# Moving the first value weights behind the last five value tiles in the load queue

## The chip, the cores and the metric

The kernel runs on one core of one Trainium2 chip. The metric is the device time of one execution in microseconds (us). The batches of experiments ran on four chips, each with the kernel before beside it in the same rounds (its medians there are 257.97 to 258.05). Below, "clock" is the TensorE clock that the profile shows as granted, as a share of full speed.

## The reference, cut to what matters

The reference runs windowed attention with block summaries for 4 batches, 8 heads, 768 positions and head size 64, then a gated feed-forward layer on the result.

```python
v_sum = v.reshape(B, H, nb, 32, D).mean(axis=3)          # one mean per block of 32 values
a = softmax([masked q k^T | q k_sum^T + log 32])         # (cut) near keys and block summaries
x = a @ concatenate([v, v_sum])                          # attention out, 3072 x 512
g, val = x @ w_gate, x @ w_val                           # 512 -> 1536 each
ffn = (gelu(g) * val) @ w_out                            # 1536 -> 512
out = x + sigmoid(x @ w_res) * ffn
```

The block means need every value of a batch. So the first attention output, and with it the first feed-forward matmul, cannot be had before the whole of the first batch's v is on the chip.

## The kernel before

Every load goes through one queue, whose DMAs GpSimd (POOL) issues. The loads cast from float32 to bfloat16. v comes as 12 tiles of 64 positions (64 KB each as landed), the gate and value weights as six chunks each (256 KB each as landed).

```python
def v_loads(b, lo=0, hi=NT):
    for t in range(lo, hi):
        nc.gpsimd.dma_start(out=vext[b % 2][0:QT, t, :, 0:D],
                            in_=v[b, :, t * QT:(t + 1) * QT, :].rearrange("h p d -> p h d"))
def load_w(c):                                   # 256 columns, two feed-forward groups
    sl = slice(c * 256, (c + 1) * 256)
    nc.gpsimd.dma_start(out=w_gate[:, :, sl], in_=wg_src[:, :, sl])
    nc.gpsimd.dma_start(out=w_val[:, :, sl], in_=wv_src[:, :, sl])
# ... k, q, then:
v_loads(0, 0, 6)
# ... four selects on POOL
v_loads(0, 6, 7)
load_w(0)
v_loads(0, 7, NT)
# ...
for c in range(1, 6):
    load_w(c)
    if c == 4:
        q_sb[1] = load_q(1, QJ)
# then w_res (residual weights), w_out (three pieces)
```

On TensorE (PE) the head of the program runs in this order. `vsum_mm` makes the block means, two matmuls for each value tile. `keep_warm(n)` issues n matmuls whose result nobody reads.

```python
s_step(0, 2, st)
s_step(0, 3, st, MM2)
vsum_mm(0, vs, 3, 7)                 # tiles 3 to 6
keep_warm(2)
# ...
for hp in range(3):
    av_first(hp, st, ao[hp], 0, BAND)   # attention matmuls, 12 for each head pair
vsum_mm(0, vs, 7, 10)
av_first(3, st, ao[3], 0, BAND)
vsum_mm(0, vs, 10, NT)
nc.vector.tensor_copy(vblk[...], vs[0][...])   # the means; then the rest of attention
# ... then transposes, and the first gate and value matmuls
```

The softmax here doesn't subtract the row's maximum and nothing guards it: scores larger than these inputs give would overflow.

Of the kernel before, what the change touches and what calls it, by code (L numbers as in the profile page):

```python
# [15 lines left out]
def kernel(  # L16
# [11 lines left out]
    nc = tc.nc  # L28
# [11 lines left out]
    NT = S // QT  # L40
# [40 lines left out]
    w_gate = wpool.tile([128, KO, DFF], BF16, name="w_gate")  # L81
    w_val = wpool.tile([128, KO, DFF], BF16, name="w_val")
# [11 lines left out]
    def load_q(half, j):  # L94
        t = qk.tile([TU // j, H, j, D], BF16, tag="q_sb", name="q_sb")
        nc.gpsimd.dma_start(
            out=t.rearrange("p h j d -> p h (j d)"),
            in_=q[0, :, half * TU:(half + 1) * TU].rearrange("h (p j) d -> p h (j d)", j=j))
        return t
# [5 lines that stand above are left out]
# [30 lines left out]
    with tc.manual_schedule():  # L135
# [20 lines left out]
        wg_src = moe_w_gate.rearrange("(ko ki) f -> ki ko f", ki=128)  # L156
        wv_src = moe_w_val.rearrange("(ko ki) f -> ki ko f", ki=128)

        def load_w(c):
            sl = slice(c * 256, (c + 1) * 256)  # L160
            nc.gpsimd.dma_start(out=w_gate[:, :, sl], in_=wg_src[:, :, sl])
            nc.gpsimd.dma_start(out=w_val[:, :, sl], in_=wv_src[:, :, sl])

        nc.vector.memset(warm[:], 0.0)
        nc.vector.memset(ident[:], 0.0)
# [15 lines left out]
        for cols, sign, base in ((slice(0, QT), 1, WIN - 1), (slice(0, QT), -1, WIN - 1),  # L181
# [2 lines left out]
            nc.gpsimd.affine_select(out=m, in_=m, compare_op=ALU.is_ge, fill=-240000.0, base=base,  # L184
                                    pattern=[[-sign, cols.stop - cols.start]], channel_multiplier=sign)
        v_loads(0, 6, 7)
        load_w(0)
        v_loads(0, 7, NT)
        kw_consts(0)
        own_keys(bmat, NT)  # L190
# [1 line left out]
        nc.vector.memset(vext[1][0:QT, :, :, D + 1:VP], 0.0)  # L192


        for c in range(1, 6):
            load_w(c)
            if c == 4:
                q_sb[1] = load_q(1, QJ)
        nc.gpsimd.dma_start(out=w_res[:], in_=moe_w_res.rearrange("(ko ki) f -> ki ko f", ki=128))
        wo_src = moe_w_out.rearrange("(fo ki) f -> ki fo f", ki=128)  # L200
        for c in range(3):
            sl = slice(c * 4, (c + 1) * 4)
# [58 lines left out]
        def vsum_mm(b, vs, lo, hi):  # L261
            for t in range(lo, hi):
                for i in range(2):
                    nc.tensor.matmul(vs[i][96:128, 0:DM // 2], bmat[:, t, :],
                                     vext[b % 2][0:QT, t, 4 * i:4 * i + 4, 0:D],
                                     start=(t == 0), stop=(t == NT - 1))
# [36 lines left out]
        def s_step(u, hp, st, banks=None):  # L303
            if banks:
                s = [p.tile([128, 512], F32, tag=tag, name="s") for p, tag in banks]
            else:
                s2 = ps_s.tile([128, 2, 512], F32, tag="s", name="s")
                s = [s2[:, hh] for hh in range(2)]
            s_mm(u, hp, [x[:, 0:TU] for x in s])
            P = ppool.tile([128, 2, HT, QT], BF16, tag="P", name="P")  # L310
            if banks:
                for hh in range(2):
                    nc.scalar.activation(P[:, hh].rearrange("p t q -> p (t q)"), s[hh][:, 0:TU], AF.Exp,  # L313
                                         scale=scale, bias=bias_t[:])
            else:
                nc.scalar.activation(P.rearrange("p a t q -> p a (t q)"), s2[:, :, 0:TU], AF.Exp,  # L316
                                     scale=scale, bias=bias_t[:])
            if u or hp > 1:
                Pf = P.rearrange("p a t q -> p (a t) q")
                nc.vector.tensor_mul(Pf, Pf, maskt.unsqueeze(1).to_broadcast([128, 2 * HT, QT]))  # L320
            st["P", hp] = P
# [17 lines left out]
        def av_first(hp, st, ao, lo, hi):  # L339
            P = st["P", hp]  # L340
            for sub in range(NSUB):
                for hh in range(2):
                    for e in range(2):
                        t, h = 2 * sub + e, 2 * hp + hh
                        rhs = vblk[lo:hi, h, :] if lo else vext[0][0:hi, t, h, 0:D + 1]
                        nc.tensor.matmul(ao[64 * e:64 * e + 64, sub, hh, :], P[lo:hi, hh, t, :], rhs,
                                         start=(lo == 0 and sub == 0 and hh == 0), stop=(lo > 0),
                                         skip_group_check=True)
# [102 lines left out]
        def keep_warm(n):  # L451
            wp = ps_s.tile([128, 2, 512], F32, tag="s", name="wp")
            for _ in range(n):
                nc.tensor.matmul(wp[:, 0], warm[:, 0:128], warm[:], start=True, stop=True)
# [16 lines left out]
        vs = [ps_t.tile([128, 512], F32, tag="t", name="vs"), ps_o.tile([128, 512], F32, tag="ao", name="vs")]  # L471
# [5 lines left out]
        vsum_mm(0, vs, 0, 3)  # L477
        s_step(0, 2, st)
        s_step(0, 3, st, MM2)
        vsum_mm(0, vs, 3, 7)  # L480
        keep_warm(2)
        gvT = upool.tile([128, FO, TU], BF16, tag="gvT", name="gvT")
        ao = [ps_mm.tile([128, NSUB, 2, D + 1], F32, tag="mm", name="ao") for _ in range(NP)]
        for hp in range(3):
            av_first(hp, st, ao[hp], 0, BAND)
        vsum_mm(0, vs, 7, 10)
        av_first(3, st, ao[3], 0, BAND)
        vsum_mm(0, vs, 10, NT)
        nc.vector.tensor_copy(vblk[96:128, 0:H // 2, 0:D],
                              vs[0][96:128, 0:DM // 2].rearrange("p (h d) -> p h d", d=D))  # L490
        nc.scalar.copy(vblk[96:128, H // 2:H, 0:D],
# [206 lines left out]
```

## Time and profile before

| what | value |
|---|---|
| time | 258.22 us, median of 3 (257.93 to 259.48) |
| profiled span | 256.2 us, clock 1.00 |
| value tiles 7 to 11 land | 17.21, 17.63, 18.05, 18.53, 18.94 us |
| first gate / value weights land | 15.46 / 16.78 us |
| first gate matmul | 22.21 us |

From the page (busy time of an engine and its share; granted clock in 40 slices; the chain that ended last, by engine):

```profile
span 256.2 us, 5835 instructions
PE 250.3 (98%) x2304; PEld 138.9 (54%) x2304; DVE 158.4 (62%) x349; ACT 127.3 (50%) x213; POOL 110.4 (43%) x155
PEclk9999999999999999999999999999999999999999
PE 88%; DMA 5%; ACT 2%; POOL 2%; DVE 2%; issue 1%; POOLq 0%; DVEq 0%
```

PE is the limit almost everywhere, so the 5% of DMA is the interesting part. The chain of waits from 3 to 22 us shows where it lies (start, duration, what; "..." marks rows left out, here and below):

```profile
3.19 7.11 DMA q_sb<-in_q_dram
10.31 0.28 issue
10.59 0.77 POOL w_gate L161
11.36 0.74 POOL w_val L162
12.10 1.34 POOL vext L103 x2
13.44 4.61 DMA vext<-in_v_dram
...
18.09 0.38 PE vs L264 x2
18.47 0.31 PE ao L346 x12
18.78 0.48 PE vs L264 x3
...
19.29 0.45 DVE vblk L489
...
22.21 0.32 PE g L374
```

The value tiles (`vext`) set the pace until 18.05 us. The timeline of PE for the same stretch (start, duration, line, what, shapes, count, idle time before):

```profile
14.80 1.04 PE L264 MATMUL vs<-vext,bmat 64*32 64x256 bf16 x8
16.05 0.59 PE L454 MATMUL wp<-warm 128*128 128x512 bf16 x2 [0.21 <-ACT P L316]
16.57 0.76 PE L346 MATMUL ao<-vext,P 96*64 96x65 bf16 x36
17.26 1.20 PE L264 MATMUL vs<-vext,bmat 64*32 64x256 bf16 x6
18.40 0.38 PE L346 MATMUL ao<-vext,P 96*64 96x65 bf16 x12
18.71 0.65 PE L264 MATMUL vs<-vext,bmat 64*32 64x256 bf16 x4
```

Eight of the block-mean matmuls take 1.04 us at 14.80. The six at 17.26 take 1.20, because they wait inside the row for one landing after another. The view prints idle time from 0.15 us up. A record lasts 0.27 us, so of each wait (0.29 us from tile 7's last matmul to tile 8's first, where the usual spacing is 0.11) almost nothing is left between the records.

A DMA's row on POOL is its issue alone (752 ns for the first value weights, which land 5.4 us after its start). A landing is the start of its issue plus the time to landing in the view of one tile. Here are the first value weights (first pair of lines), then value tiles 7 to 11 (second pair):

```profile
L162 POOL DMA_DIRECT2D w_val<-in_moe_w_val_dram x1: 752/752/752, 11.3 to 11.3; - x1
DMA to landing us min/median/max: 5.4/5.4/5.4
...
L103 POOL DMA_DIRECT2D vext<-in_v_dram x5: 713/722/1042, 12.1 to 15.1; - x5
DMA to landing us min/median/max: 3.9/4.6/5.1
```

The value weights land at 16.78 us, 5.6 us before the first value matmul (22.38) reads them, and the tiles that PE is waiting for queue behind them.

### The profile page before, as it was taken

The numbers are of one execution on the slowest core, as the hardware profiler recorded it, in microseconds if no ns is written. First come the engines' busy times: TensorE is split into PE (matmuls) and PEld (weight loads), VectorE is DVE, ScalarE is ACT, GpSimd is POOL, SyncE is SP. The second block draws the span as 40 slices with busy tenths as digits, with TensorE's granted clock in tenths as the row PEclk, the third lists the DMA queues.
The fourth block names the chain that finished last, engine by engine and source line by source line (L and its number), as shares of the span: only waits on it lengthen the run. The fifth ranks groups of instructions, "written<-read, shape, count | busy, mean of one in ns | idle before, by whom it ended". The sixth has DMA issues, their size and how long they took to land.

```text
span 256.2 us, 5835 instructions
## 1 busy us (share of the span) xinstructions
PE 250.3 (98%) x2304; PEld 138.9 (54%) x2304; DVE 158.4 (62%) x349; ACT 127.3 (50%) x213; POOL 110.4 (43%) x155
## 2 busy tenths in 40 slices
PE   7999999999999999999999999999999999999994
PEld 2555664565654565545554565545554665555543
DVE  5965776389467544767667544777567544854424
ACT  6667359356483337344493338344482338253320
POOL 8898533193344888255405987076404000000000
PEclk9999999999999999999999999999999999999999
DMA  5999999999903999979704999969803500240003
GB/s 80 178 159 168 197 202 207 186 155 176 141 20 82 175 110 144 127 137 175 131 3 100 168 107 146 117 130 180 135 15 70 144 0 3 50 139 0 0 3 123
DMA packets 98475, 29.34 MB, mean 115 GB/s; under 512 B 83592, under 2 KB 95312, under 8 KB 98352
## 3 DMA queue, kind: packets, MB, share of 16 engines
q0 software_dynamic: 68720, 14.76, 70.1%
q1 hardware_dynamic: 29728, 14.21, 26.1%
q8 instruction: 18, 0.29, 0.5%
q14 instruction: 9, 0.07, 0.2%
HBM read 29.36 MB, written 6.29 MB: 139 GB/s over the span
## 4 chain that ended last, share of the span: by engine, by line
PE 88%; DMA 5%; ACT 2%; POOL 2%; DVE 2%; issue 1%; POOLq 0%; DVEq 0%
PE g L374 25%; PE vv L374 24%; PE f L422 24%; PE r L412 7%; DMA q_sb<-in_q_dram 3%; PE ao L334 3%; PE s L298 2%; DMA vext<-in_v_dram 2%; PE tp L210 1%; PE vs L272 1%; DVE o L431 1%; DVE th L428 1%; POOL k_sb L88 1%; POOL vext L103 1%; PE xp L359 1%
## 5 line engine op out<-in xcount | busy, mean ns | idle before, releaser
L380 DVE TENSOR_TENSOR gvT<-ge,vv 128x384 bf16<-128x384 f32 x96 | 52.7, 552 | 50.7 <-PE vv L374 46.3
L379 ACT ACTIVATE ge<-g 128x384 f32<-128x384 f32 x96 | 46.9, 490 | 68.6 <-DVE gvT L380 38.1
L374 PE MATMUL g<-xT,w_gate 128*128 128x384 bf16 x384 | 78.8, 326 | 0.2
L374 PE MATMUL vv<-xT,w_val 128*128 128x384 bf16 x384 | 78.7, 326 | 0.0
L422 PE MATMUL f<-w_out,gvT 128*128 128x512 bf16 x276 | 64.6, 380 | 0.0
L374 PEld LDWEIGHTS <-w_gate 128*128 128x128 bf16 x384 | 37.2, 98 | 26.5 <-issue 1.6
L374 PEld LDWEIGHTS <-w_val 128*128 128x128 bf16 x384 | 37.5, 98 | 24.8 <-issue 0.3
L422 PEld LDWEIGHTS <-gvT 128*128 128x128 bf16 x276 | 25.7, 98 | 29.2
L103 POOL DMA_DIRECT2D vext<-in_v_dram x48 | 33.4, 743 | 14.4 <-DMA w_out<-in_moe_w_out_dram 6.3
L415 ACT ACTIVATE th<-r 128x512 f32<-128x512 f32 x24 | 13.5, 605 | 27.5 <-PE r L412 27.5
L428 DVE SCALAR_TENSOR_TENSOR th<-th,f 128x512 f32<-128x512 f32 (+2 forms) x26 | 16.6, 640 | 14.0 <-PE f L422 14.0
L320 DVE TENSOR_TENSOR P<-P,maskt 128x768 bf16<-128x768 bf16 x30 | 17.1, 571 | 11.8 <-ACT P L316 6.6
L412 PE MATMUL r<-w_res,xT 128*128 128x512 bf16 x96 | 23.1, 380 | 0.0
L284 POOL COPY vext<-vsum 32x1536 bf16<-32x1536 bf16 x12 | 17.2, 1463 | 12.9 <-DMA vsum<-vpart 12.8
L431 DVE SCALAR_TENSOR_TENSOR o<-th,xn 128x512 f32<-128x512 f32 (+2 forms) x26 | 18.8, 722 | 0.9
L354 DVE TENSOR_TENSOR xn<-ao,rz 128x384 bf16<-128x384 f32 x32 | 17.8, 558 | 1.1
L117 POOL DMA_DIRECT2D k_nat<-in_k_dram x24 | 16.4, 730 | 2.9 <-DMA k_nat<-in_k_dram 2.2
L316 ACT ACTIVATE P<-s,bias_t 128x768 bf16<-128x768 f32 x17 | 15.3, 902 | 4.3 <-PE s L298 4.1
L123 POOL DMA_DIRECT2D q_nat<-in_q_dram x18 | 15.9, 921 | 0.7 <-issue 0.7
L313 ACT ACTIVATE P<-s,bias_t 128x384 bf16<-128x384 f32 x30 | 15.7, 580 | 0.0
L227 DVE TENSOR_REDUCE ks<-kW 128x24 bf16<-128x768 bf16 x16 | 15.1, 944 | 0.4 <-ACT kW L242 0.3
L412 PEld LDWEIGHTS <-xT 128*128 128x128 bf16 x96 | 8.8, 98 | 9.9
(82 smaller groups left out, 173.3 us busy)
## 6 DMA issues: line engine op xcount, KB each, us to landing
out_dram<-o SPq DMA_DIRECT2D x23, 256.0 KB, 2.3
vext<-in_v_dram POOLq DMA_DIRECT2D x48, 64.0 KB, 6.5
q_nat<-in_q_dram POOLq DMA_DIRECT2D x18, 128.0 KB, 7.3
w_gate<-in_moe_w_gate_dram POOLq DMA_DIRECT2D x6, 256.0 KB, 7.4
w_val<-in_moe_w_val_dram POOLq DMA_DIRECT2D x6, 256.0 KB, 8.0
w_out<-in_moe_w_out_dram POOLq DMA_DIRECT2D x3, 512.0 KB, 14.3
k_nat<-in_k_dram POOLq DMA_DIRECT2D x24, 64.0 KB, 5.0
vext<-vext SPq DMA_DIRECT2D x6, 144.0 KB, 5.5
```

The costliest lines, as they stand in the source:

```text
L103: nc.gpsimd.dma_start(out=vext[b % 2][0:QT, t, :, 0:D], in_=v[b, :, t * QT:(t + 1) * QT, :].rearrange("h p d -> p h d"))
L117: nc.gpsimd.dma_start(out=k_nat[:, t].rearrange("p (h d) -> p h d", d=D), in_=k[b, :, t * QT:(t + 1) * QT, :].rearrange("h p d -> p h d"))
L284: eng.tensor_copy(vext[b % 2][96:128, lo:hi, :, 0:D], src)
L320: nc.vector.tensor_mul(Pf, Pf, maskt.unsqueeze(1).to_broadcast([128, 2 * HT, QT]))
L354: nc.vector.tensor_mul(xn, ao[:, :, :, 0:D], rz.to_broadcast([128, NSUB, 2, D]))
L374: nc.tensor.matmul(ps[:, 0:TU], w[:, ko, fo * 128:(fo + 1) * 128], st["xT"][:, ko, :], start=(ko == 0), stop=(ko == KO - 1), skip_group_ch ...
L379: nc.scalar.activation(ge[:], g[:, 0:TU], AF.Gelu)
L380: nc.vector.tensor_mul(gvT[:, fo, :], ge[:], vv[:, 0:TU])
L412: nc.tensor.matmul(r[:], st["xT"][:, ko, ss], w_res[:, ko, :], start=(ko == 0), stop=(ko == KO - 1))
L422: nc.tensor.matmul(st["f", sub][:], gvT[:, fo, ss], w_out[:, fo, :], start=(fo == 0), stop=(fo == FO - 1), skip_group_check=True)
L428: nc.vector.scalar_tensor_tensor(th[:, cs], th[:, cs], 1.0, f[:, 0:n], ALU.add, ALU.mult)
L431: nc.vector.scalar_tensor_tensor(o.rearrange("p (k d) -> p k d", d=128), th[:, cs].rearrange("p (k d) -> p k d", d=128), 0.5, x, ALU.mult, ...
```

## The change

The first value weights go behind all value tiles, and the first gate weights stay in front of the last five. On PE, the block means of tile 7 move ahead of the two warm-up matmuls and the later ones are regrouped to match.

```diff
-        def load_w(c):
+        def load_w(w, src, c):
             sl = slice(c * 256, (c + 1) * 256)
-            nc.gpsimd.dma_start(out=w_gate[:, :, sl], in_=wg_src[:, :, sl])
-            nc.gpsimd.dma_start(out=w_val[:, :, sl], in_=wv_src[:, :, sl])
+            nc.gpsimd.dma_start(out=w[:, :, sl], in_=src[:, :, sl])
         v_loads(0, 6, 7)
-        load_w(0)
+        load_w(w_gate, wg_src, 0)
         v_loads(0, 7, NT)
...
-        for c in range(1, 6):
-            load_w(c)
+        for c in range(6):
+            if c:
+                load_w(w_gate, wg_src, c)
+            load_w(w_val, wv_src, c)
...
-        vsum_mm(0, vs, 3, 7)
+        vsum_mm(0, vs, 3, 8)
         keep_warm(2)
...
-        vsum_mm(0, vs, 7, 10)
+        vsum_mm(0, vs, 8, 11)
         av_first(3, st, ao[3], 0, BAND)
-        vsum_mm(0, vs, 10, NT)
+        vsum_mm(0, vs, 11, NT)
```

## The prediction

> What bounds the kernel now. From about 22 us to the end, TensorE: the page gives PE 98% of a 256.2 us span, the chain of waits is 88% PE, and the timeline of PE after 22.2 us has one idle stretch over 0.15 us (0.22 us at 43.15). So only what starts the feed-forward matmuls sooner can count, and that is the head. There the chain runs through the load of q, the issues on POOL of the first gate and value weights (10.59, 11.36) and of value tiles, then 4.61 us of "DMA vext" until 18.05, then PE.
>
> Landings (issue plus time to landing, tile by tile) come in the order of issue: value tile 6 at 14.48, first gate chunk 15.46, first value-weight chunk 16.78, value tiles 7 to 11 at 17.21, 17.63, 18.05, 18.53, 18.94. [...] PE waits for these tiles: the block-mean matmuls (L264) of tiles 7, 8, 9 start at 17.26, 17.67, 18.09, within 0.05 us of their landings, the last of tile 11 at 19.09. The value weights put ahead are first read at 22.38, 5.6 us after landing.
>
> What the change does. No work is added or removed. One 256 KB transfer, 16.78 - 15.46 = 1.32 us of the queue, goes behind five value tiles; each of these is issued 0.75 us sooner. Issuing costs the same (0.75 us for weights, 0.7 for a tile, 1.0 while VectorE copies rims at 13.7 to 15.8). The shortest times from the end of a tile's issue to its landing in the trace are about 2 us, so issue leaves room. I estimate landings of tiles 7 to 11 at 15.9, 16.3, 16.75, 17.2, 17.6, about 1.3 us sooner, and of the first value weights at 19 to 19.5, still 2.5 us before use. Later weights should land within 0.5 us of before.
>
> How much is critical. Not 1.3 us, because PE becomes the limit. Forward with the trace's own spacing (0.11 us a block-mean matmul): tile 7 at 15.93, two warm-up matmuls to 16.6, 36 attention matmuls to 17.25, tiles 8 to 10 to 18.0 without a wait, 12 attention matmuls to 18.3, tile 11's last start at about 18.55, against 19.09: 0.54 us gained. From there to the first gate matmul (22.21) runs a chain of VectorE, PE and ACT that should move as a whole, to about 21.67. Later loads have slack: last value-weight chunk lands 35.99, read at 37.35; residual weights 38.53 against 39.85. So the gain should stay to the end.
>
> Predicted: 258.22 - 0.54 = 257.7 us, range 257.1 to 258.4 (three runs before: 257.93 to 259.48). Faster by over 2%: 0.01; within 2%: 0.98; slower: 0.01.
>
> What would show each step. Right: value tiles about 1.3 us sooner and 0.43 us apart; no wait of L264 for vext except tile 7; last L264 start near 18.55; first gate matmul near 21.7; the same shift at 40 us and at the end. Wrong: tile 11 landing after 18.4 because POOL's issue limits it; tile 7 landing after 16.2, which delays everything behind it, since its matmuls now stand before the warm-up ones; first value weights after 21.8 and a wait at the first value matmul; a new wait for weights at 36 to 40 us that gives the gain back; a shift at 22 us that does not reach the end.

The order of the loads in the queue is taken from the landings in the trace of before.

## The result, and the profile after

The changed kernel took 257.56 us (median of 6, 257.50 to 257.64), the kernel before in the same rounds 258.01 us (median of 6, 257.92 to 259.48). The medians differ by 0.45 us. The ratio is 0.9973 (95% interval 0.9951 to 0.9994). A ratio here is the mean time of one kernel's fast runs over that of the other's in the same rounds. So it is not the ratio of the medians (0.9983): the mean of before contains its one run at 259.48.

The page after:

```profile
span 255.7 us, 5810 instructions
PE 247.6 (97%) x2279; PEld 138.7 (54%) x2304; DVE 157.5 (62%) x349; ACT 127.4 (50%) x213; POOL 110.5 (43%) x155
PE 91%; ACT 3%; DMA 2%; DVE 2%; issue 1%; POOLq 0%; DVEq 0%
```

The lower count of PE is records missing from the trace (the program has the same 2304 matmuls; weight loads, recorded in full, are 2304 in both). It is not less work. The chain of waits no longer passes through a value tile:

```profile
16.05 0.57 DVE P L321
16.62 0.12 issue
16.74 0.76 PE ao L347 x36
17.50 0.76 PE vs L265 x6
18.25 0.31 PE ao L347 x12
18.56 0.22 PE vs L265
...
18.81 0.44 DVE vblk L490
...
21.74 0.32 PE g L375
```

The row of VectorE (DVE), the masking of P, is an inference of this view. Without the warm-up matmuls (an experiment below) the attention matmuls start at 16.23 us, so the mask does not hold their start.

The timeline of PE after (these lines of the program are one further down, and one of the two warm-up matmuls is among the missing records):

```profile
14.82 1.46 PE L265 MATMUL vs<-vext,bmat 64*32 64x256 bf16 x10
16.20 0.39 PE L455 MATMUL wp<-warm 128*128 128x512 bf16 x1
16.74 0.76 PE L347 MATMUL ao<-vext,P 96*64 96x65 bf16 x36
17.43 0.82 PE L265 MATMUL vs<-vext,bmat 64*32 64x256 bf16 x6
18.18 0.38 PE L347 MATMUL ao<-vext,P 96*64 96x65 bf16 x12
18.49 0.39 PE L265 MATMUL vs<-vext,bmat 64*32 64x256 bf16 x2
...
21.90 0.32 PE L375 MATMUL vv<-xT,w_val 128*128 128x384 bf16 x1
```

The six block-mean matmuls at 17.43 now take 0.82 us instead of 1.20: nothing waits inside. The last one starts at 18.61 us (before: 19.09), the first gate matmul at 21.74 (before: 22.21). Every later gate matmul is 0.48 us earlier too, at 38 us, 114 us and 241 us alike.

The landings in the changed kernel (first value weights, then value tiles 7 to 11):

```profile
L161 POOL DMA_DIRECT2D w_val<-in_moe_w_val_dram x1: 1074/1074/1074, 15.1 to 15.1; - x1
DMA to landing us min/median/max: 5.0/5.0/5.0
...
L103 POOL DMA_DIRECT2D vext<-in_v_dram x5: 699/709/981, 11.4 to 14.1; - x5
DMA to landing us min/median/max: 3.5/3.9/4.4
```

Tile by tile the value tiles land at 15.86, 16.27, 16.69, 17.12 and 17.59 us, 1.35 us sooner than before, and the first value weights at 20.06.

So the tiles came 1.35 us sooner and the kernel became 0.45 us shorter. The experiments ask what became of the rest, which half of the change did it, and what else the change moved.

### The profile page after: what moved, and what is told of

Its sections match the earlier page's. It is cut to its first block, busy times and chain, and to the rows that moved or that the text cites. A ratio compares the mean times of both kernels' runs of the same rounds, so it can differ in the third digit from the quotient of the medians.

```text
span 255.7 us, 5810 instructions
## 1 busy us (share of the span) xinstructions
PE 247.6 (97%) x2279; PEld 138.7 (54%) x2304; DVE 157.5 (62%) x349; ACT 127.4 (50%) x213; POOL 110.5 (43%) x155
## 4 chain that ended last, share of the span: by engine, by line
PE 91%; ACT 3%; DMA 2%; DVE 2%; issue 1%; POOLq 0%; DVEq 0%
PE g L375 25%; PE vv L375 24%; PE f L423 23%; PE r L413 7%; PE ao L335 3%; PE s L299 2%; DMA k_sb<-in_k_dram 2%; PE tp L211 2%; PE wp L455 1%; ACT P L317 1%; PE vs L273 1%; PE ao L347 1%; ACT P L314 1%; DVE o L432 1%; DVE th L429 1%
## 5 line engine op out<-in xcount | busy, mean ns | idle before, releaser
L423 PE MATMUL f<-w_out,gvT 128*128 128x512 bf16 x262 | 62.7, 379 | 1.3 <-issue 1.0
L285 POOL COPY vext<-vsum 32x1536 bf16<-32x1536 bf16 x12 | 17.2, 1464 | 14.1 <-DMA vsum<-vpart 13.9
L123 POOL DMA_DIRECT2D q_nat<-in_q_dram x18 | 15.9, 917 | 0.7 <-issue 0.7
```

Source lines behind the costliest of these rows:

```text
L285: eng.tensor_copy(vext[b % 2][96:128, lo:hi, :, 0:D], src)
L423: nc.tensor.matmul(st["f", sub][:], gvT[:, fo, ss], w_out[:, fo, :], start=(fo == 0), stop=(fo == FO - 1), skip_group_check=True)
```

## The experiments

Theory 1: before, the landings of the last value tiles bind. After, PE's own order of work does, so most of the earlier landing is slack. Its main rival, theory 2: the regrouping on PE made the difference. Medians are of six executions (five in one case), those of the kernel before of eleven from the same rounds.

### The order of the loads alone

```diff
 (after)
-        vsum_mm(0, vs, 3, 8)    ... 8, 11 ... 11, NT
+        vsum_mm(0, vs, 3, 7)    ... 7, 10 ... 10, NT
```

> The order of the loads as after, the block-mean matmuls of tiles 7 to 11 grouped on PE as before (3 to 6, then 7 to 9, then 10 and 11). Theory 1 (the earlier landings are the gain; the regrouping only fills PE's wait before 16.05 us): landings as after (tile 11 at 17.6), last block-mean matmul starts at about 18.7 (after 18.61, before 19.09), whole kernel 0.4 us under before, so at most 0.1 us slower than after. Theory 2 (the regrouping on PE is what shortened it): last start near 19.0 or later, whole kernel within 0.1 us of before.

Measured: 257.62 us against 258.03 for before, ratio 0.9975 (0.9954 to 0.9996). That is 0.41 us under before by the medians, where the whole change gave 0.45. Its profiled execution was the second slowest of the six (257.78): PE is 0.17 us behind the changed kernel's from the transposes of k at 8.85 us on, ahead of anything that the edit touches. So its last block-mean matmul at 18.86 stands for about 18.7 in an ordinary execution, an estimate from that offset. The order of the loads is nearly the whole gain (the 0.04 us that are left are within the spread of the executions), and theory 2 falls.

### The regrouping alone

```diff
 (before)
-        vsum_mm(0, vs, 3, 7)    ... 7, 10 ... 10, NT
+        vsum_mm(0, vs, 3, 8)    ... 8, 11 ... 11, NT
```

> The order of the loads as before, the block-mean matmuls grouped as after (tile 7 ahead of the two warm-up matmuls). Theory 1: tile 7 still lands at 17.2, so warm-up and attention matmuls now stand behind it; last block-mean matmul at about 19.95, whole kernel about 0.85 us slower than before. Theory 2: 0.1 to 0.5 us faster than before.

Measured: 262.02 us against 258.03, nearly five times the loss that I expected. PE waited for tile 7 as foreseen (1.31 us), but then the granted clock was 0.50 and a warm-up matmul took 0.61 us, where one in before took 0.39. The timeline of PE, and then the busy time of the engines in two stretches (columns after the stretch: its length, PE, PEld, DVE, ACT, POOL, then clock, DMA share, GB/s):

```profile
17.35 0.58 PE L264 MATMUL vs<-vext,bmat 64*32 64x256 bf16 x2 [1.31 <-DMA vext<-in_v_dram]
17.86 0.61 PE L454 MATMUL wp<-warm 128*128 128x512 bf16 x1
...
13.70:17.10 3.40, 2.34 (x50) 1.68 (x43) 2.64 (x4) 3.40 (x7) 3.40 (x5) 1.00 1.84 175
17.10:20.50 3.40, 2.79 (x42) 1.71 (x43) 0.56 (x1) 0.05 (x1) 3.40 (x5) 0.50 1.45 146
```

The trace's clock records have it at 0.5 for 10.24 us, from 17.11 to 27.35. Neither theory had this, so I repeated the run with the wait filled.

### The regrouping alone, with the wait filled

```diff
 (before, regrouped)
-        vsum_mm(0, vs, 3, 8)
+        vsum_mm(0, vs, 3, 7)
+        keep_warm(6)
+        vsum_mm(0, vs, 7, 8)
```

> The run before (grouping alone) waited 1.4 us for tile 7 and then ran 10.2 us at a granted clock of 0.5, which made it 4 us slower, not 0.85. Here the same grouping on the old order of loads, with six more warm-up matmuls (0.22 us each) ahead of tile 7's, to fill that wait. Theory 1 with the clock as the cause of the excess: granted clock 1.0 throughout the head, last block-mean matmul at 19.9 to 20.1, whole kernel 0.8 to 1.0 us over before. Rival (something else in the grouping costs 4 us, such as the order of the accumulation): 3 us or more over before, with the clock at 1.0.

Measured: 259.10 us against 257.97, so 1.13 us over before, all six executions within 258.98 to 259.13 and at a clock of 0.998 or more. The last block-mean matmul starts at 20.18, a little later than foreseen. So the regrouping by itself costs about 1 us, and the other 3 us of the run above (262.02 us, at a mean clock of 0.979 to 0.987) went with the clock. The regrouping is right only together with the new order of loads.

### The gate weights behind the tiles as well

```diff
 (after)
         v_loads(0, 6, 7)
-        load_w(w_gate, wg_src, 0)
         v_loads(0, 7, NT)
...
-            if c:
-                load_w(w_gate, wg_src, c)
+            load_w(w_gate, wg_src, c)
```

> After, with the first gate weights behind the last five value tiles too. Theory 1 (PE is the limit from the moment tile 7 is there, and the exp that frees the PSUM of the warm-up matmuls comes at 16.02): value tiles land 0.7 to 1.0 us sooner still, but only PE's wait for tile 7 (0.2 us) is left to gain: last block-mean matmul 18.45 to 18.5, first gate matmul about 21.6, whole kernel 0.1 to 0.15 us under after, provided the first gate weights land before 21.6 (expected 18.5 to 20) and the residual weights before 39.2. Rival (the gain is in proportion to the landings): another 0.3 us or more. Other rival (gate weights are needed in front): they land after 21.6 and PE waits for them, slower than after.

Measured: the tiles landed at 14.58 to 16.39 us, another 1.2 to 1.4 us sooner, and the first gate matmul started at 21.59, only 0.15 us sooner than in the changed kernel. That is as theory 1 says: PE binds. But the whole kernel took 257.86 us (257.50 to 258.57), no faster than the changed kernel's 257.56. In the profiled execution the 0.15 us is lost again between 36 and 38 us, where the last value weights land at 36.81 and their matmul starts at 36.86. My expectation of the total was wrong here. The head had become shorter, and the stream of weights behind it later: the residual weights landed at 39.33 us, against 39.08 in the changed kernel and 38.53 before. The profiled execution is the fastest of the six (257.50), and the slowest is 1.07 us longer. No trace of a slow one was taken, so its cause stays open.

### The changed kernel without two warm-up matmuls

```diff
 (after)
         vsum_mm(0, vs, 3, 8)
-        keep_warm(2)
```

> After, without the two warm-up matmuls between the block-mean and the attention matmuls. Theory 1 (PE's own order of work is the limit there now): attention matmuls start at about 16.2, those of the third head pair wait for the masked P until 16.65, last block-mean matmul at about 18.25 instead of 18.61, whole kernel about 0.3 us under after; at 39 us the residual weights (landing 39.1) come near to a wait. Rival (still bound by the landings of the value tiles, or the two matmuls keep the clock up): same time as after, or slower with granted clock below 1.

Measured: the last block-mean matmul started at 18.15 us instead of 18.61, and the first gate matmul at 21.27 instead of 21.74. Removing PE work from the head shortened the head at once, so PE does bind there. The clock stayed at 0.999 or more. The whole kernel gained less: 257.41 us (257.05 to 258.35). The profiled execution (257.57) shows where the gain went. From its timeline of PE (the last block-mean matmuls, then the wait) and its chain of waits:

```profile
18.03 0.39 PE L265 MATMUL vs<-vext,bmat 64*32 64x256 bf16 x2
...
36.85 0.82 PE L375 MATMUL vv<-xT,w_val 128*128 128x384 bf16 x4 [0.28 <-DMA w_val<-in_moe_w_val_dram]
...
24.99 11.82 DMA w_val<-in_moe_w_val_dram
```

Its gate matmuls are 0.46 us ahead of the changed kernel's up to 37 us, and level with them (0.02 us ahead) from 38 us on. In this execution all of it was given back in one wait for the last value weights. No trace shows whether the faster ones (down to 257.05) escaped that wait.

### Before without the same two warm-up matmuls

```diff
 (before)
         vsum_mm(0, vs, 3, 7)
-        keep_warm(2)
```

> Before, without the same two warm-up matmuls. Theory 1 (before is bound there by the landings of tiles 7 to 11, after by PE's own work): tiles land as in before (17.2 to 18.9), the last block-mean matmul still starts at 19.0 to 19.1, whole kernel within 0.1 us of before, while the same removal brought the first gate matmul of after 0.47 us forward. Rival (PE bound in both): 0.4 us faster than before. If the missing matmuls cost the clock, granted clock 0.5 shows for some 10 us and it is 3 us or more slower.

Measured: the value tiles landed as in before and the last block-mean matmul started at 19.06 us (before 19.09):

```profile
18.66 0.67 PE L264 MATMUL vs<-vext,bmat 64*32 64x256 bf16 x4
```

Removing the same PE work moved nothing there, so in before the landings bind. That is the other half of theory 1. But the total was 260.53 us, and five of the six executions had a mean clock of 0.986 to 0.993. The one at full clock took 257.96 us, the time of before. In the profiled execution the clock is at 0.5 from 19.40 to 26.23 us.

### One more chunk in front of the tiles

```diff
 (before)
         load_w(0)
+        nc.gpsimd.dma_start(out=w_gate[:, :, 256:512], in_=wg_src[:, :, 256:512])
         v_loads(0, 7, NT)
```

(Its later load is taken out.)

> Before, with the second gate chunk put in front of the last five value tiles as well (a dose in the other direction). Theory 1 (before is bound by the landings): tile 11 lands 1.3 us later, at about 20.2, last block-mean matmul at about 20.4, whole kernel 1.3 us slower if the clock stays at 1.0; PE then waits 1.3 us for tile 7, about as long as where the clock fell to 0.5, and in that case 4 to 6 us slower. Rival (the place of one chunk in the queue matters little, the gain of after came from elsewhere): within 0.3 us of before.

Measured: 262.81 us (five executions) against 257.97, at a mean clock of 0.980 to 0.987. The tiles landed at 18.57 to 21.39, the last block-mean matmul started at 21.60, and the clock fell to 0.5 from 21.23 to 28.06. The direction and the size are those of the case with the cut clock. The last tile landed 2.45 us later than in before (21.39 against 18.94) rather than the 1.3 that I gave. I don't know why that one was late. The residual weights landed at 37.54 us, the earliest of all runs.

### The first value weights one place later still

```diff
 (after)
         for c in range(6):
             if c:
                 load_w(w_gate, wg_src, c)
-            load_w(w_val, wv_src, c)
+            if c == 1:
+                load_w(w_val, wv_src, 0)
+            if c:
+                load_w(w_val, wv_src, c)
```

> After, with the first value weights one place further back, behind the second gate chunk. They should land where that chunk landed in after, at 21.8 to 22.5, and are wanted at 21.90. Theory 1 (landing before 21.9 is all that matters of them, so the place that the change gave them is the last one that is free): a wait of 0 to 0.6 us at the first value matmul, the first place where the weights bind, and the last value weights at 36.5 absorb or add to it: 0 to 0.6 us over after. Rival (there is slack beyond): same as after within 0.05 us with no wait.

Measured: 258.04 us, 0.48 us over the changed kernel's 257.56 (each against its own rounds; the kernel before was at 257.97 and 258.01). The weights landed at 22.34, and PE waited for them:

```profile
22.39 0.34 PE L378 MATMUL vv<-xT,w_val 128*128 128x384 bf16 x1 [0.22 <-DMA w_val<-in_moe_w_val_dram]
```

The first value matmul starts 0.39 us later than it would have right behind the first gate matmul; another 0.10 us had been lost before that in this execution (first gate matmul at 21.84). One place further back costs all that the change had gained. In this order of loads the place that the change chose is the last free one.

### Before, with its short waits filled

The executions of the kernel before. In the rounds of the experiments, 12 of 44 took 259.25 to 261.49 us at a mean clock of 0.986 to 0.993. The other 32 took 257.88 to 258.30 at 0.997 or more. (Of the six in the rounds of the result, one more took 259.48.)

```diff
 (before)
-        vsum_mm(0, vs, 7, 10)
+        for t in range(7, 10):
+            vsum_mm(0, vs, t, t + 1)
+            keep_warm(1)
```

> Before, with one warm-up matmul (0.22 us) put behind the block-mean matmuls of each of tiles 7, 8 and 9, in the waits for the next tile. So far 11 of 39 executions of before took 259.4 to 261.5 us with a mean granted clock of 0.986 to 0.993, and none of the executions of after or of those kernels whose PE stays fed there did. Theory (in before the waits for the tiles let the load of PE fall [...]): all executions at a clock of 0.997 or more, none over 258.6, the median within 0.2 us of before's undisturbed 258.0, since the landings still bind. Rival (the outliers come from outside, such as a neighbour on the chip): about a quarter of these executions at 0.993 and 259.5 too.

What the run tests is whether the lower clocks go with before's waits for tiles 7 to 11.

Measured: 258.72 us (258.69 to 259.04), every execution at 0.998 or more. The clock part of the expectation held, and the time did not: the three fills did not fit into the waits, and PE ran 0.7 us late. At a share of 12 in 44, six undisturbed executions out of six would still come by chance about one time in seven. So this run alone supports the theory and does not settle it. The other runs say more against the rival: in the same rounds 54 executions of kernels whose PE does not wait for tile after tile (the changed kernel again, the order alone, the filled grouping, the gate weights behind, without warm-ups after, one place later, the faster version twice, and this one) were all at 0.997 or more. A cause from outside would hardly have spared them all. Twelve of them (the filled grouping and this one) have before's order of loads, so that order by itself is not the cause either.

### The changed kernel again

> The changed kernel once more, unaltered, on the chip of this batch. Expected: median 257.5 to 257.7, 0.4 to 0.5 us under the undisturbed executions of before, none of its executions at a clock under 0.997, while about a quarter of those of before are. Rival for the last point: one or two of six here too.

Measured: 257.54 us (257.45 to 257.72), no execution under 0.998. Before in the same rounds had two of eleven at 0.991 and 0.993. With the first six that makes 12 executions of the changed kernel, all within 257.45 to 257.72, all at full clock. In its profiled execution, the slowest of the 12 at 257.72 us, the last value weights landed at 37.02 and the gate matmuls lost 0.1 us there: the new limit was touched.

### A faster version, twice

The experiment without the two warm-up matmuls showed one wait that gave the gain back. In this version the first unit runs its last two gate groups ahead of its last two value groups, as the other units do already. The residual weights come in four pieces that are used piece by piece.

```diff
 (after)
-        keep_warm(2)
...
-                elif u and fo == FO - 2:
+                elif fo == FO - 2:
                     fo_last_two(st, gvT)
-                elif u == 0 or fo < FO - 2:
+                elif fo < FO - 2:
...
-        nc.gpsimd.dma_start(out=w_res[:], in_=...)
+        for ko in range(KO):
+            nc.gpsimd.dma_start(out=w_res[:, ko], in_=wr_src[:, ko])
...  (in first_out)
-            for sub in range(NSUB):
-                res_step(st, sub)
+            # three r tiles; for ko: for sub: matmul; then the three tanh
```

> After, without the two warm-up matmuls (which brought the first gate matmul 0.47 us forward but gave 0.45 us back at 36.9 us, in a wait for the last value weights, landing 36.80), and with that wait moved away: in the first unit the last two gate groups run ahead of the last two value groups, and the residual weights come in four pieces whose matmuls go piece by piece. Theory (the gain was given back at the landing of these weights and nowhere else): no wait over 0.1 us at 36 to 40 us, the shift of 0.4 to 0.5 us against after reaches the end, 257.1 us. Rival (the time is lost elsewhere, or the stream of weights as a whole binds, so that the wait only moves to the next chunk): 257.4 us or more, with a new wait at the gate weights (35.5) or at the output weights (41.9).

> The version without the two warm-up matmuls and with the waits for the last weights moved away, once more, beside after on the same chip. Expected: median 257.1, 0.4 to 0.5 us under after of the same rounds, no execution with a lower clock. Rival: the former result was one chip's luck, and it is within 0.2 us of after or shows a cut clock.

Measured: 257.13 us the first time (257.07 to 257.22) and 257.14 us the second, against 257.54 for the changed kernel of the same rounds. So it is about 0.4 us faster than the changed kernel and beats both. The changed order and the split of the residual weights were not tried one by one. In its first profiled execution no wait over 0.1 us is left between 36 and 40 us. But two of the second six took 257.96 and 258.21 us at full clock, and the profiled one shows why: the first value weights landed at 22.45 us, not 19.56, and PE waited 0.9 us for them. The version lives close to the landing of those weights and is less steady than the changed kernel. Its mean of twelve is 257.28 against 257.56.

## Why the prediction was right

The time was right: 257.7 predicted, 257.56 measured, inside the range and within 2%. That alone proves little. The range also holds the unchanged kernel (258.01), and two small errors partly cancelled: the base of 258.22 was 0.21 us over that of the rounds, and the gain was put 0.09 us too high. What tests the prediction is the head of the trace.

The mechanism was right. The tiles were expected at 15.9, 16.3, 16.75, 17.2 and 17.6 us, and they landed at 15.86, 16.27, 16.69, 17.12 and 17.59. PE then became the limit. The last block-mean matmul was put at 18.55 and started at 18.61. The first gate matmul was put at 21.67 and started at 21.74. The gain was put at 0.54 us and measured 0.45. The pair of runs without the two warm-up matmuls shows the switch of the limit directly: the same removal moves the last block-mean matmul by 0.03 us in before and by 0.46 us in after. The run with the gate weights behind shows that still earlier tiles bring only 0.15 us.

Three points missed: the weights behind the tiles, the slack that is left, and the clock.

"I estimate landings ... of the first value weights at 19 to 19.5": they landed at 20.06. "Later weights should land within 0.5 us of before": the last value weights landed 0.54 us later (36.53 against 35.99) and the residual weights 0.55 (39.08 against 38.53). Two others missed by more, with slack enough that PE did not wait: the second gate chunk landed 0.73 us later (22.21 against 21.48) and the fifth value chunk 1.32 (32.38 against 31.06). I had taken the queue as filled. But a value tile takes 0.7 us to issue, and tiles that stand in the queue land only about 0.43 us apart (0.41 to 0.48 in before). From these two figures I estimate that POOL does not keep the queue full with tiles alone, and that the 1.3 us of weights in front of them had been the backlog. Over all the runs, the landing of the residual weights goes with the number of chunks in front of the last five tiles:

| chunks in front | residual weights land (us) |
|---|---|
| 0 | 39.33 |
| 1 (the changed kernel, its repeat, and three experiments) | 38.90 to 39.56 |
| 2 (before and four experiments) | 38.18 to 38.88 |
| 3 | 37.54 |

Each of these is one profiled execution; the faster version is left out, because it loads the residual weights in pieces. The ranges for one and two chunks touch (38.90 and 38.88), and the value for none lies inside the range for one, so the trend is plain only from one end of the table to the other.

That the queue ran thinner can be read in the traces. The view of stretches (columns as above; the last is GB/s) from 15 to 20 us, before and then after:

```profile
15.00:20.00 5.00, 4.63 (x84) 2.77 (x84) 2.40 (x4) 2.53 (x6) 5.00 (x8) 1.00 1.71 152
...
15.00:20.00 5.00, 4.73 (x113) 3.19 (x113) 2.65 (x6) 3.03 (x6) 5.00 (x8) 1.00 1.51 139
```

With three chunks in front the same stretch has 174 GB/s, with none 130. That POOL's issues are what thins the queue is my estimate from the issue and landing times above, and that this makes up the whole 0.55 us is not shown.

Slow issues may add to it. In both kernels two of POOL's issues take about 1.0 us instead of 0.7 while VectorE copies the rims of the tiles (13.7 to 15.8 us). In before these are tiles 10 and 11 (0.98 and 1.04 us), with the weights still in the queue in front of them. After, they are tile 11 and the first value weights themselves (0.98 and 1.07 us). That the copies are what slows these issues is not shown: the copies last about 1.0 us each and the issues grew by 0.3, and the issue of tile 9 in before (13.44 to 14.16 us) overlaps the first copy by 0.4 us and took 0.72. In the slow execution of the faster version the issues of tiles 10 and 11 took 1.25 and 1.06 us, and the value weights behind them landed 2.9 us later than in its fast one. But their own issue ended only 0.58 us later (16.57 against 15.99), so most of these 2.9 us stays unexplained.

"So the gain should stay to the end" held, but with less to spare than I said. I gave the last value weights 1.36 us of slack (35.99 to 37.35) and the residual weights 1.32. After the change both are wanted 0.48 us sooner and land 0.55 later, so about 0.3 us of either is left. The next gain in the head of 0.46 us ran into exactly that wait.

What I did not think of was the clock. Before, PE waited for one tile after another around 17 to 19 us, and 12 of 44 executions had a cut clock; 11 of them took about 1.5 us more and one 3.5. The changed kernel had none in 12, which at that share would come by chance about one time in 45. For the kernels that were profiled in that state (the regrouping alone, before without warm-up, one more chunk in front) the cut is seen to start in the stretch in which PE waited for value tiles or right behind it, at 17.11, 19.40 and 21.23 us. The busy time of PE does not tell these cases apart by itself: in the 3.4 us ahead of the cut PE was busy for 2.34, 3.01 and 1.76 us, and the changed kernel without warm-up matmuls kept a clock of 1.00 through 3.42 us (17.50 to 20.92) with 2.95 busy. Why only some executions of before are cut is not shown. For before itself no execution with a cut clock was profiled. So that its waits are the cause is likely, not shown.

## What to carry to other kernels

In one queue whose loads land in the order of their issue, as here (in before 15.46, 16.78, then 17.21 to 18.94 us), put a load by when it is first read, and check two ends: what the moved load was holding back, and when it is itself wanted. Here one place too early cost 0.4 us and one place too late cost 0.5. A landing that comes 1.35 us sooner is worth only the distance to the next limit, so work the next limit out from the spacing of the engine's own instructions before hoping for more. And after such a gain, look at the slack of all later loads: it shrank here from 1.3 us to 0.3, and the next improvement was lost in it until the order of use was changed there too.
